# One attention-and-feed-forward kernel: a pinned TensorE order, a reordered first chunk, matmuls on zeros during the first loads, and a regrouped broadcast of the denominators

## The chip, the cores and the metric

The kernel runs on one core of one Trainium2 chip. The metric is device time in microseconds (us), smaller is better; a kernel is run several times and the median is quoted.

A ratio is the mean time of one kernel's runs over the mean of the other kernel's runs of the same rounds on the same chip, so it is not quite the ratio of the medians that stand beside it. Below 1 is faster than the kernel before.

Names used by the profile: PE is TensorE (matmuls), DVE is VectorE, ACT is ScalarE, POOL is GpSimd, SP the engine that issues most loads. A trailing "q" (ACTq, POOLq) is the sequencer of that engine, where it issues a DMA.

## The reference, cut to what matters

```python
def reference(A_x, A_wqkv, A_wo, B_x, B_w_gate, B_w_up, B_w_down, c, w_mod):
    # x: 1 x 2048 x 1024; 32 heads of 32; F = 3584; all bf16
    mod = (silu(c) @ w_mod)              # six rows of 1024: sa, ca, ga, sb, cb, gb
    h = layernorm(x) * (1 + ca) + sa
    q, k, v = heads(h @ wqkv)
    pq, pk = phi(q), phi(k)              # phi(t) = where(t > 0, t + 1, exp(t)) + 1e-6
    kv = einsum('bhsd,bhse->bhde', pk, v)
    z = einsum('bhsd->bhd', pk)
    den = einsum('bhqd,bhd->bhq', pq, z) + 1e-6
    o = einsum('bhqd,bhde->bhqe', pq, kv) / den
    x = x + ga * (o @ wo)
    h = layernorm(x) * (1 + cb) + sb
    return x + gb * ((silu(h @ w_gate) * (h @ w_up)) @ w_down)
```

The attention is linear. Every query needs only the sum over all keys (`kv`, `z`), so K and V of all tokens come before any output. Each query and head is divided by one number, `den`.

## The kernel before

The 2048 tokens are handled as four chunks of 512, called K0, V0, Q0 and so on below. A scheduler decides the order of instructions on each engine when the program is built, unless the program tells it otherwise; an engine then keeps to that order. The parts that the change and the argument touch:

```python
# loads, all issued by SP, in this order: c, four x tiles, then per half b of the contraction
for b in range(2):
    for q in (1, 0):
        t = big("wme", [DC, NB])                       # modulation weights of this half
        nc.sync.dma_start(out=t[:], in_=wm_v[:, :, q * D + b * NB:q * D + (b + 1) * NB])
    for i in range(2):
        nc.sync.dma_start(out=wk[b][:, 2 * i:2 * i + 2, :], in_=wqkv_v[...])
# ... cut: wv follows after K0, wq only in chunk 2 ...

def phi_to(dst, acc):                                  # evacuates one PSUM bank of K or Q
    e = ep.tile([P, NB], BF16, name="eb")
    nc.scalar.activation(out=e[:], in_=acc, func=ACT.Exp)
    nc.vector.tensor_scalar(out=e[:], in0=e[:], scalar1=1.0, scalar2=PHI_EPS, op0=ALU.min, op1=ALU.add)
    nc.vector.scalar_tensor_tensor(out=dst, in0=acc, scalar=0.0, in1=e[:], op0=ALU.max, op1=ALU.add)

def q_phase(sc, lo=0, hi=DC):
    for qc in range(lo, hi):
        acc = acc_a()                                  # one of four PSUM banks
        for cc in range(DC):
            nc.tensor.matmul(acc[:], lhsT=wq[...], rhs=hTs[sc][:, cc, :], ...)
        phi_to(pqs[sc][:, qc, :], acc[:])

def den_norm(sc):
    # ... cut: 32 small matmuls give den, VectorE takes its reciprocal rb (128 x 128),
    #     four small DMAs write rb to rden_dram ...
    rbc = big("rbc", [HG, SCW])                        # 128 x 8 x 512 bf16, 1 MB
    rv = rden_dram[sc].rearrange("(g h) t -> h g t", h=HPC)
    for h in range(HPC):                               # HPC = 4, DH = 32
        nc.gpsimd.dma_start(out=rbc[h * DH:(h + 1) * DH, :, :],
                            in_=rv[h].unsqueeze(0).to_broadcast([DH, HG, SCW]))

def den_apply(sc):
    for k in range(4):
        ks = slice(2 * k, 2 * k + 2)
        nc.vector.tensor_tensor(out=pq[:, ks, :], in0=pq[:, ks, :], in1=rbc[:, ks, :], op=ALU.mult)

# order: K0 V0 K1 KV0 K1 V1 ... K3 V3, then
q_phase(0, 0, 2); kv_phase(3); q_phase(0, 2, 8); q_phase(1, 0, 1)
den_norm(0); den_apply(0)
# ... cut: rest of Q1, four output tiles (a_ps), Q2, Q3, den_norm(1), den_norm(2) ...
# then per chunk: gate/up (wgu) and down (wd), with the next chunk's output tiles in between
```

The denominators go out to DRAM and come back as a broadcast: each of the 32 rows of one head position is written to 32 partitions. That is what `rbc` is.

## Time and profile before

| | before |
|---|---|
| median of 3 runs | 859.06 us (858.94 to 859.39) |
| span of the profiled run | 856.0 us |
| TensorE busy | 832.5 us, 97% |
| V of chunk 0 ends | 56.6 us |
| gate/up of chunk 0 starts | 229.8 us |

The head of the page of before: the span, TensorE's busy time, and the clock row (40 slices of the span, granted clock in tenths).

```profile
span 856.0 us, 10310 instructions
...
PE 832.5 (97%) x4236; PEld 383.4 (45%) x4236; DVE 322.1 (38%) x621; ACT 141.1 (16%) x239; POOL 45.4 (5%) x125
...
PEclk9999999999999999999999999999999999999999
```

TensorE bounds the kernel. What can be won is what it loses, most of it before 57 us. Next is the timeline of TensorE of before. Its columns are start, duration, engine, line, operation, output and inputs, count, and in brackets the idle time just before with what ended it.

```profile
10.36 1.89 PE L175 MATMUL tp<-ident,xn 128*128 128x128 bf16 x16 [10.36 <-DVE xn L166]
...
20.82 1.44 PE L237 MATMUL acc<-wk,hT 128*128 128x512 bf16 x3
22.91 1.02 PE L207 MATMUL mod_ps<-scT,wme 128*128 128x1 bf16 x32 [0.66 <-DMA wme<-in_w_mod_dram]
23.79 12.77 PE L237 MATMUL acc<-wk,hT 128*128 128x512 bf16 x45
37.70 3.61 PE L237 MATMUL acc<-wk,hT 128*128 128x512 bf16 x16 [1.14 <-DVE pk L222]
41.83 3.20 PE L251 MATMUL acc<-wv,hT 128*128 128x512 bf16 x14 [0.51 <-DMA wv<-in_A_wqkv_dram]
45.81 10.95 PE L251 MATMUL acc<-wv,hT 128*128 128x512 bf16 x50 [0.79 <-DMA wv<-in_A_wqkv_dram]
```

TensorE idles for 10 us, starts the first half of K only behind the second block of modulation matmuls, and later waits for wv. The K matmuls also run slowly at first. The following are the groups of the K line in two short stretches of before; the three durations are the shortest, median and longest in ns.

```profile
L237 PE MATMUL acc<-wk,hT x3: 587/634/634, 20.8 to 21.6; 128*128 128x512 bf16 x3
...
L237 PE MATMUL acc<-wk,hT x11: 379/379/380, 29.7 to 31.9; 128*128 128x512 bf16 x11
```

The same matmul lasts 634 ns at first and 379 ns from 29.7 us on: the array is cold, then warm. The clock row does not show it.

Three more views of before matter later; they show how the broadcast travels. First the tile view of `rbc`: the issues, and from issue to landing (shortest, median, longest).

```profile
L348 POOL DMA_DIRECT2D rbc<-rden_scratch x16: 583/588/622, 173.8 to 294.4; - x16
...
DMA to landing us min/median/max: 4.1/8.9/12.9
```

Then the table of windows while the first four broadcasts run. The last three columns are the granted clock, the mean busy share of the core's 16 DMA engines, and GB/s.

```profile
178.00:179.00 1.00, 1.00 (x6) 0.47 (x5) 0.60 (x1) 1.00 (x3) 0.00 (x0) 1.00 1.02 221
```

All 16 engines are busy. Last, the timeline of VectorE at the multiply that uses the broadcast.

```profile
186.86 2.49 DVE L356 TENSOR_TENSOR pq<-pq,rbc 128x1024 bf16<-128x1024 bf16 x4
```

The multiply at 186.86 has no wait in brackets. The data were there, and seven Q evacuations had been placed between the reciprocal (169.5 us) and this multiply.

### The profile page before, as it was taken

How to read it: one execution, taken by the hardware profiler on the slowest of the kernel's cores; microseconds unless marked ns; L12 is line 12 of the kernel's file. 1: busy time of each engine (PE TensorE's matmuls, PEld its weight loads, DVE VectorE, ACT ScalarE, POOL GpSimd, SP SyncE). 2: the span in 40 equal slices, each digit the busy share in tenths (PEclk: the TensorE clock that was granted, in tenths of full speed). 3: DMA queues.
4: the chain of work that ended last, by engine and by line, in shares of the span. 5: the costliest groups of instructions: out<-in, count | busy, mean ns of one | idle time of the engine just before them, and what ended most of it. 6: DMA issues, size and time to landing. Idle time of an engine off the chain costs nothing.

```text
span 856.0 us, 10310 instructions
## 1 busy us (share of the span) xinstructions
PE 832.5 (97%) x4236; PEld 383.4 (45%) x4236; DVE 322.1 (38%) x621; ACT 141.1 (16%) x239; POOL 45.4 (5%) x125
## 2 busy tenths in 40 slices
PE   3899999999999999999999999999999999999997
PEld 2344444544444444444444444444444444444443
DVE  5884532658613333542211155211224532211122
ACT  2223333351311110001111100011110001111000
POOL 2110000012210100100000011000000100000000
PEclk9999999999999999999999999999999999999999
DMA  9699900028995492738344073483503629720011
GB/s 302 232 218 303 319 6 1 1 51 222 297 249 175 120 337 66 222 90 258 122 140 155 1 215 106 145 267 104 165 32 103 186 87 294 234 80 1 18 56 38
DMA packets 126478, 128.72 MB, mean 150 GB/s; under 512 B 33632, under 2 KB 107488, under 8 KB 126432
## 3 DMA queue, kind: packets, MB, share of 16 engines
q1 hardware_dynamic: 122208, 115.36, 45.1%
q0 software_dynamic: 3840, 12.65, 4.7%
q8 instruction: 33, 0.54, 0.3%
q10 hardware_dynamic: 384, 0.07, 0.0%
q14 instruction: 13, 0.11, 0.0%
HBM read 108.01 MB, written 12.71 MB: 141 GB/s over the span
## 4 chain that ended last, share of the span: by engine, by line
PE 91%; DMA 3%; DVE 3%; SPq 2%; POOL 0%; issue 0%; ACT 0%; DVEq 0%; POOLq 0%
PE acc L464 45%; PE acc L484 23%; PE acc L251 6%; PE a_ps L428 5%; PE acc L237 5%; PE acc L262 5%; DMA wv<-in_A_wqkv_dram 1%; SPq L114 1%; DMA x_sb<-in_A_x_dram 1%; PE kvp L273 1%; SPq L110 1%; DMA x_scratch<-x_1999 1%; DVE xn L166 1%; DVE stats L162 0%; POOL rstd L156 0%; PE modr L298 0%
## 5 line engine op out<-in xcount | busy, mean ns | idle before, releaser
L464 PE MATMUL acc<-h2T,wgu 128*128 128x512 bf16 x1792 | 387.4, 379 | 0.0
L464 PEld LDWEIGHTS <-wgu 128*128 128x128 bf16 x1792 | 175.3, 98 | 211.3
L484 PE MATMUL acc<-wd,gu 128*128 128x512 bf16 x896 | 196.3, 379 | 0.0
L470 DVE TENSOR_TENSOR gu<-acc,e 128x512 bf16<-128x512 f32 x112 | 77.5, 692 | 299.0 <-PE acc L464 294.3
L469 ACT ACTIVATE e<-acc 128x512 f32<-128x512 f32 x112 | 66.8, 597 | 502.5 <-PE acc L464 502.5
L484 PEld LDWEIGHTS <-gu 128*128 128x128 bf16 x896 | 87.7, 98 | 105.7
L237 PE MATMUL acc<-wk,hT 128*128 128x512 bf16 x256 | 60.6, 395 | 1.1 <-DVE pk L222 1.1
L487 DVE TENSOR_TENSOR e<-acc,gb_bc 128x512 f32<-128x512 f32 x32 | 22.1, 692 | 104.2 <-PE acc L484 104.2
L262 PE MATMUL acc<-hT,wq 128*128 128x512 bf16 x256 | 57.2, 379 | 1.0 <-DVE pq L222 1.0
L428 PE MATMUL a_ps<-wo,pq 128*128 128x512 bf16 x256 | 57.8, 379 | 0.1
L251 PE MATMUL acc<-wv,hT 128*128 128x512 bf16 x256 | 56.1, 379 | 1.3 <-DMA wv<-in_A_wqkv_dram 1.3
L220 ACT ACTIVATE eb<-acc 128x512 bf16<-128x512 f32 x64 | 37.8, 598 | 100.9 <-PE acc L237 48.9
L221 DVE TENSOR_SCALAR eb<-eb 128x512 bf16<-128x512 bf16 x64 | 18.5, 294 | 61.6 <-ACT eb L220 61.4
L237 PEld LDWEIGHTS <-hT 128*128 128x128 bf16 x256 | 25.3, 101 | 32.8 <-issue 6.0
L251 PEld LDWEIGHTS <-hT 128*128 128x128 bf16 x256 | 25.0, 98 | 31.9 <-issue 1.1
L262 PEld LDWEIGHTS <-wq 128*128 128x128 bf16 x256 | 24.9, 98 | 30.7 <-issue 1.2
L428 PEld LDWEIGHTS <-pq 128*128 128x128 bf16 x256 | 24.8, 98 | 30.8 <-DVE pq L356 1.5
L254 ACT CAST v<-acc 128x512 bf16<-128x512 f32 x32 | 18.7, 585 | 37.8 <-PE acc L251 37.8
L489 DVE TENSOR_TENSOR ob<-e,x1r 128x512 bf16<-128x512 f32 x32 | 22.1, 692 | 1.1
L222 DVE SCALAR_TENSOR_TENSOR pq<-acc,eb 128x512 bf16<-128x512 f32 x32 | 21.9, 690 | 0.8
L162 DVE BATCH_NORM_STATS2 stats<-x_sb 128x6 f32<-128x512 bf16 x32 | 20.7, 668 | 4.0 <-DMA x_sb<-in_A_x_dram 4.0
L222 DVE SCALAR_TENSOR_TENSOR pk<-acc,eb 128x512 bf16<-128x512 f32 x32 | 21.7, 687 | 0.5
(130 smaller groups left out, 245.9 us busy)
## 6 DMA issues: line engine op xcount, KB each, us to landing
wgu<-in_B_w_gate_dram SPq DMA_DIRECT2D x28, 1024.0 KB, 6.4
wgu<-in_B_w_up_dram SPq DMA_DIRECT2D x28, 1024.0 KB, 8.9
x_sb<-in_A_x_dram SPq DMA_DIRECT2D x32, 256.0 KB, 5.0
wml<-in_w_mod_dram SPq DMA_DIRECT2D x8, 1024.0 KB, 9.8
x1r<-x_scratch SPq DMA_DIRECT2D x32, 256.0 KB, 3.0
wd<-in_B_w_down_dram SPq DMA_DIRECT2D x7, 1024.0 KB, 14.3
wme<-in_w_mod_dram SPq DMA_DIRECT2D x4, 1024.0 KB, 10.6
rbc<-rden_scratch POOLq DMA_DIRECT2D x16, 256.0 KB, 8.9
```

The source lines that it names most:

```text
L220: nc.scalar.activation(out=e[:], in_=acc, func=ACT.Exp)
L222: nc.vector.scalar_tensor_tensor(out=dst, in0=acc, scalar=0.0, in1=e[:], op0=ALU.max, op1=ALU.add)
L237: nc.tensor.matmul(acc[:], lhsT=hTs[sc][:, cc, t * P:(t + 1) * P], rhs=wk[cc // 4][:, cc % 4, nb * NB:(nb + 1) * NB], start=(cc == 0), sto ...
L251: nc.tensor.matmul(acc[:], lhsT=hTs[sc][:, cc, t * P:(t + 1) * P], rhs=wv[cc // 4][:, cc % 4, nb * NB:(nb + 1) * NB], start=(cc == 0), sto ...
L262: nc.tensor.matmul(acc[:], lhsT=wq[cc // 4][:, cc % 4, qc * P:(qc + 1) * P], rhs=hTs[sc][:, cc, :], start=(cc == 0), stop=(cc == DC - 1))
L428: nc.tensor.matmul(a_ps[:], lhsT=pq[:, hg, t * P:(t + 1) * P], rhs=wo[hg // 4][:, hg % 4, ns], start=(hg == 0), stop=(hg == HG - 1))
L464: mm = nc.tensor.matmul(acc[:], lhsT=w[:, cc, fj * P:(fj + 1) * P], rhs=h2Ts[sc][:, cc, :], start=(cc == 0), stop=(cc == DC - 1))
L469: nc.scalar.activation(out=sg[:], in_=ps[0][:], func=ACT.Silu)
L470: gm = nc.vector.tensor_tensor(out=guT[sc][f // GPT][:, f % GPT, :], in0=ps[1][:], in1=sg[:], op=ALU.mult)
L484: nc.tensor.matmul(y_ps[:], lhsT=guT[sc][f // GPT][:, f % GPT, t * P:(t + 1) * P], rhs=wd[f // WDF][:, f % WDF, ns], start=(f == 0), stop= ...
L487: nc.vector.tensor_tensor(out=yt[:], in0=y_ps[:], in1=gb_bc[:, ns], op=ALU.mult)
L489: nc.vector.tensor_tensor(out=ob[:], in0=yt[:], in1=x1r[:], op=ALU.add)
```

## The change

The intent is to fill the start. wv and wq are queued early, K0 is split by halves of the contraction so that its first half runs before the second modulation block, Q0 comes right after V0, and matmuls on a zero tile (48 of them, results never read) keep the array warm while loads arrive. TensorE's stream is pinned to the order of the program, so that the scheduler cannot undo this. Layer normalisation of the later chunks moves from VectorE to ScalarE, the x1 stores from GpSimd's queue to ScalarE's. Along with it, the four broadcasts of the denominators become one, with a new order of rows in the scratch buffer.

```diff
+    def mm(out, lhsT, rhs, start, stop):
+        return tc.keep_in_program_order(nc.tensor.matmul(out, lhsT=lhsT, rhs=rhs, start=start, stop=stop))
 # ... cut: every matmul and transpose goes through mm / transpose ...
+        if b == 0:
+            load_x(STC - 1, nc.sync)
+    wv = load_w(wqkv_v, 2 * D, "wv")
+    for st in range(STC, 2 * STC):
+        load_x(st, nc.sync)
+    wq = load_w(wqkv_v, 0, "wq")
 # ... cut ...
-                nc.gpsimd.memset(zmask[rs, hg, HPC * hg + h:HPC * hg + h + 1], 1.0)
+                nc.gpsimd.memset(zmask[rs, hg, HG * h + hg:HG * h + hg + 1], 1.0)
 # ... cut: normalise_act, ln1 and modulate split into parts ...
         rbc = big("rbc", [HG, SCW])
-        rv = rden_dram[sc].rearrange("(g h) t -> h g t", h=HPC)
-        for h in range(HPC):
-            nc.gpsimd.dma_start(out=rbc[h * DH:(h + 1) * DH, :, :],
-                                in_=rv[h].unsqueeze(0).to_broadcast([DH, HG, SCW]))
+        rv = rden_dram[sc].rearrange("(h g) t -> h (g t)", h=HPC)
+        nc.gpsimd.dma_start(out=rbc[:].rearrange("p g t -> p (g t)"),
+                            in_=rv.unsqueeze(1).to_broadcast([HPC, DH, HG * SCW]))
 # ... cut ...
+    def keep_warm(acc, n):
+        for _ in range(n):
+            mm(acc[:], lhsT=sel[:, 0, :], rhs=sel[:], start=True, stop=True)
+    keep_warm(accs[5], 26)
+    with in_order(nc.vector, nc.scalar, nc.gpsimd):
+        # ... cut: normalise and transpose tiles 0 to 2, keep_warm(accs[5], 4) after each ...
+        for b in range(2):
+            mod_block(b, 1)
+            keep_warm(idle, 2)
+            mod_block(b, 0)
+            keep_warm(idle, 3)
+            # ... cut: modulate ...
+            if b == 0:
+                k_mms(0, gs, accs, 0, 4)            # first half of the contraction
+                # ... cut: fourth tile ...
+            else:
+                k_mms(0, gs, accs, 4, 8)
 # ... cut ...
         v_phase(sc)
         if sc + 1 < NSC:
-            ln1(sc + 1, True)
-            modulate_all(hTs[sc + 1], ca1T, saT)
+            with tc.issue_after(last_on[nc.vector.engine]):
+                ln1(sc + 1)
+                modulate_all(hTs[sc + 1], ca1T, saT)
+        if sc == 0:
+            q_phase(0)
 # ... cut: the later Q chunks are redistributed, den_norm(1) moves ahead of the output tiles ...
-        nc.gpsimd.dma_start(out=x1_dram[st * P:(st + 1) * P, :], in_=x1[:])
+        nc.scalar.dma_start(out=x1_dram[st * P:(st + 1) * P, :], in_=x1[:])
```

## The prediction

> **What bounds the kernel.** TensorE: the header of the page has it busy 832.5 of 856.0 us. Counting its matmuls at the steady start-to-start spacing of the timeline (448 gate/up matmuls in 96.7 us, 0.216 us each) I get about 827 us of work; with 4.4 us of tail after the last matmul that leaves roughly 24 us that any reordering could win. The timeline of TensorE says where they are: the first transpose starts at 10.36 us, and V of chunk 0 ends at 56.6 us, when only about 35 us of that work is done: 21 us lost before 56.6, about 2.5 us after it (waits of 1.0 us at 215.6, 0.8 us at 229.6, and smaller ones).
>
> Three losses make up the first part that can move. (a) The first half of K (24 matmuls, 5.2 us warm) could run from about 16 us, when the first modulation blocks are in, but in the stream it stands behind the second block: only 3 K matmuls start before 23.8 us. (b) From 20.8 to 29.5 us the K matmuls last 634 ns each, later 379 ns: the array is cold. The Trainium skill, "TensorE: Matmul & The Clock Gate", Part 1, says that the clock is halved until about 3.4 us of sustained activity; the trace agrees (634 against 379 ns), although the page's PEclk row shows full clock. That costs about 2.7 us. (c) Stalls of 1.1 us at 37.7 (a PSUM bank not yet evacuated), and 0.5 and 0.8 us for wv, which was issued only at 36.45 us, behind x loads that waited for buffers, while the DMA row was nearly empty from 27 to 36 us.
>
> **What the change does.** wv and wq are queued right behind wk. With 350 to 380 GB/s wv lands near 31 us. The fourth x tile goes behind the first wk half. The last modulation block still lands at about 22.8 us, because the same bytes are ahead of it; this is the wall. After it: 32 small matmuls 0.9, copy and first modulate 0.5, so the second K half starts at about 24.5, ends at 29.7; the two remaining groups 3.5: K ends near 33.2 (41.3 before). V then needs 13.8 us: it ends at 47.0 instead of 56.6. Q0 follows with wq long present, while the normalisation of chunk 1 finishes near 53 us. The 48 zero matmuls lie in idle time, except about 0.6 us just before the second K half. So **-9.6 us**, all on the critical path.
>
> Q0 only moves, no work is saved. Later stalls: the two near 215 and 230 us go (-1.7); pinning removes the freedom to slip ready matmuls in front of waiting ones: I allow +1 to +2 us, at the transposes of KV (only 16 matmuls ahead of them), at the first attention-output tile (waits for the denominators' round trip, 20 us before, 19.6 us of work now), and at the first gate weights (19.6 us after the output tiles, 28 before). Normalisation moved to ScalarE is off the path.
>
> **Prediction: 849.0 us, range 846 to 852.5.** Faster by over 2% 0.03, within 2% 0.96, slower 0.01.
>
> **Right or wrong.** Timeline of TensorE: V of chunk 0 ends at 47 (45.5 to 49); K matmuls at 379 ns from the first; second K half starts at 24 to 25.5, set by the landing of the last modulation block; no wait for wv. Steady gate/up and down stretches unchanged. TensorE busy grows by the zero matmuls.
>
> **What would make it wrong.** Zero matmuls that do not keep the clock up, or that overrun the first transposes (26 cold ones could last to 9 us); a slower DMA start; head-of-line waits of several us at the three places above, since nothing can slip past them.

## The result, and the profile after

| | before | after |
|---|---|---|
| median of 4 runs each | 859.0 us (858.02 to 859.39) | 881.3 us (879.47 to 881.36) |
| ratio, 95% interval | | 1.0256 (1.0238 to 1.0274) |
| span of the profiled run | 856.0 | 879.6 |
| V of chunk 0 ends | 56.6 | 47.7 |
| gate/up of chunk 0 starts | 229.8 | 247.4 |
| gate/up of chunk 1 starts | 388.7 | 412.2 |

The changed kernel is slower by 2.6%. Up to V0 it is 8.9 us ahead; at the first gate/up matmul it is 17.6 us behind. Most of these 26.5 us are lost between 187 and 240 us. The head of the page of after:

```profile
span 879.6 us, 10369 instructions
...
PE 840.3 (96%) x4201; PEld 387.4 (44%) x4284; DVE 306.7 (35%) x602; ACT 173.9 (20%) x267; POOL 37.0 (4%) x124
...
PEclk9999999989799999999999999999999999999999
```

TensorE's busy time grew (zero matmuls, and matmuls on a cold array), and the clock row now dips in its 9th and 11th slices, that is from 176 to 198 and from 220 to 242 us. The timeline of TensorE of after:

```profile
1.21 8.33 PE L98 MATMUL acc<-sel 128*128 128x512 bf16 x26 [1.21 <-DVE sel L390]
...
16.22 5.35 PE L98 MATMUL acc<-wk,hT 128*128 128x512 bf16 x24
...
25.20 8.81 PE L98 MATMUL acc<-wk,hT 128*128 128x512 bf16 x39
33.84 13.98 PE L98 MATMUL acc<-wv,hT 128*128 128x512 bf16 x63
47.66 7.07 PE L98 MATMUL acc<-hT,wq 128*128 128x512 bf16 x31
57.61 8.73 PE L98 MATMUL acc<-hT,wq 128*128 128x512 bf16 x31 [2.88 <-DVE pq L262]
...
198.35 0.58 PE L98 MATMUL acc<-hT,wq 128*128 128x512 bf16 x1 [10.40 <-DVE pq L262]
...
201.34 13.98 PE L98 MATMUL a_ps<-wo,pq 128*128 128x512 bf16 x63
...
230.58 5.83 PE L98 MATMUL acc<-hT,wq 128*128 128x512 bf16 x16 [8.36 <-DVE pq L262]
238.15 3.61 PE L98 MATMUL acc<-hT,wq 128*128 128x512 bf16 x16 [1.74 <-DVE pq L262]
...
247.44 55.42 PE L98 MATMUL acc<-h2T,wgu 128*128 128x512 bf16 x251
```

The start is as intended: both halves of K and all of V run without a gap. Then there are four waits, all said to be for VectorE's evacuation of Q (`pq`): 2.88, 10.40, 8.36 and 1.74 us. The matmuls after the first three waits are cold (those after the last, 16 in 3.61 us, are not): the 32 after 57.61 (31 of them recorded) take 8.73 us where the 32 before took 7.07. Half clock shows in the windows of after for the long waits (0.50 in the stretch from 192 to 194 us).

Why was VectorE late with Q? Its own timeline of after answers for the 10.40 us:

```profile
179.31 0.69 DVE L262 SCALAR_TENSOR_TENSOR pq<-acc,eb 128x512 bf16<-128x512 f32 x1
194.87 2.50 DVE L388 TENSOR_TENSOR pq<-pq,rbc 128x1024 bf16<-128x1024 bf16 x4 [14.86 <-DMA rbc<-rden_scratch]
```

VectorE stands at the multiply for 14.86 us, waiting for the broadcast; the Q evacuations placed behind it in its stream cannot pass, the four PSUM banks of Q fill, and TensorE stands too. The tile view of `rbc` of after gives the transfer:

```profile
L380 POOL DMA_DIRECT2D rbc<-rden_scratch x4: 700/710/715, 175.5 to 310.3; - x4
...
DMA to landing us min/median/max: 19.3/23.8/29.0
```

and the windows of after give the load on the DMA engines while it runs:

```profile
182.00:184.00 2.00, 2.00 (x11) 0.90 (x10) 0.00 (x0) 1.68 (x4) 0.00 (x0) 1.00 0.25 61
```

One transfer of 1 MB takes 19.3 us at best, with a DMA share of 0.25. A quarter of 16 engines is four engines (the view gives only the mean share; that it is four fully busy ones is a reading, which e5 supports). In before the same megabyte went as four transfers with a share of about 1. The second wait has the same root, by a longer way. These are lines of the chain that ended last, in order of time: start, duration, what.

```profile
175.51 19.33 DMA rbc<-rden_scratch
...
211.59 15.71 DMA x1r<-x_scratch
...
227.38 0.33 ACTq L515
```

The second broadcast was issued at 205.4 us, right ahead of the x1 stores and the first x1 reload. That reload (256 KB) took 15.71 us, against a median of 3.0 in the same kernel. ScalarE's queue waited for it before it issued the fourth x1 store at 227.38, so ScalarE's Exp, and with it the Q evacuations, stood still. That is the 8.36 us.

### The profile page after: what moved, and what is told of

It is laid out like the page before. It is cut to its first block, busy times and chain, and to the rows that moved or that the text cites. A ratio compares the mean times of both kernels' runs of the same rounds, so it can differ in the third digit from the quotient of the medians. Undisturbed runs are those within 1.5% of the kernel's fastest.

```text
span 879.6 us, 10369 instructions
## 1 busy us (share of the span) xinstructions
PE 840.3 (96%) x4201; PEld 387.4 (44%) x4284; DVE 306.7 (35%) x602; ACT 173.9 (20%) x267; POOL 37.0 (4%) x124
## 4 chain that ended last, share of the span: by engine, by line
PE 82%; DMA 11%; DVE 4%; issue 1%; ACT 1%; POOL 1%; ACTq 0%; SPq 0%; DVEq 0%; POOLq 0%
PE acc L98 75%; DMA rbc<-rden_scratch 5%; PE a_ps L98 5%; DMA x1r<-x_scratch 2%; DMA wd<-in_B_w_down_dram 2%; DVE stats L198 1%; DVE pq L388 1%; DMA x_scratch<-x_2148 1%; DMA x_sb<-in_A_x_dram 1%; PE kvp L98 1%; DMA h2T<-xn 0%; DMA rden_scratch<-rb 0%; PE modr L98 0%; DVE pq L262 0%; ACT v L297 0%
## 5 line engine op out<-in xcount | busy, mean ns | idle before, releaser
L98 PE MATMUL acc<-hT,wq 128*128 128x512 bf16 x248 | 62.3, 403 | 24.1 <-DVE pq L262 23.4
L98 PE MATMUL acc<-wk,hT 128*128 128x512 bf16 x250 | 56.1, 379 | 0.3
L192 POOL TENSOR_TENSOR rstd<-veps,neg_half 128x1 f32<-128x1 f32 x32 | 17.9, 558 | 449.7 <-DVE veps L190 449.7
## 6 DMA issues: line engine op xcount, KB each, us to landing
wd<-in_B_w_down_dram SPq DMA_DIRECT2D x7, 1024.0 KB, 28.7
rbc<-rden_scratch POOLq DMA_DIRECT2D x4, 1024.0 KB, 23.8
```

The costliest lines, as they stand in the source:

```text
L98: return tc.keep_in_program_order(nc.tensor.matmul(out, lhsT=lhsT, rhs=rhs, start=start, stop=stop))
L192: nc.gpsimd.tensor_tensor(out=rstd[:, 0:n], in0=veps[:, 0:n], in1=neg_half[:].to_broadcast([P, n]), op=ALU.pow)
```

## The experiments

Each kernel is the changed kernel (after) with the edit shown, unless said otherwise. Medians are of four runs each. The kernel before, on the same chips, had medians of 858.07 (e1 to e4), 858.37 (e5 to e8) and 858.33 us (e9, e10).

The theory (A in the expectations): the single broadcast uses 4 of 16 DMA engines, lands late, and VectorE and ScalarE hold Q's evacuations behind it. It rests on the Trainium skill, "DMA: Bandwidth & Descriptors", section "Why a DMA increments its semaphore by 16 and not by 1" (the paragraph on how many engines): the number of engines is the largest number up to 16 that divides the size of the slowest dimension, other than 1, of both sides. The source is [4, 32, 4096] and the destination [128, 4096], so 4; in before it is 32 rows to 32 partitions, so 16. The trace agrees: share 0.25 against about 1. The rivals were: the x1 stores moved to ScalarE (theory B); the pin on TensorE (theory C); the fact that it is one transfer rather than four; the new 8 KB rows; and the place of the multiply in VectorE's stream. The normalisation moved to ScalarE was not tested by itself; e1 and e9 keep it and are fast, so it is not enough to cause the loss.

| run | edit in a few words | median us (range) | ratio (95%) |
|---|---|---|---|
| e1_rbc4 | broadcast as four | 853.52 (853.4–855.31) | 0.9951 (0.9936–0.9966) |
| e2_x1pool | x1 stores on GpSimd | 881.34 (879.87–881.9) | 1.0268 (1.0253–1.0283) |
| e3_rbc4_x1pool | both | 858.88 (857.55–861.37) | 1.0012 (0.9993–1.0032) |
| e4_nopin | no pin | 887.23 (884.98–890.44) | 1.033 (1.0306–1.0355) |
| e5_rbc_swap | one transfer, source dims swapped | 854.96 (852.47–857.55) | 0.9957 (0.9929–0.9985) |
| e6_late_apply | multiply placed later | 869.55 (868.48–869.88) | 1.0125 (1.011–1.014) |
| e7_before_rbc1 | before, with the one broadcast | 874.17 (871.29–875.04) | 1.0175 (1.0154–1.0196) |
| e8_rbc4_q0 | e1, Q0's evacuations first | 856.66 (854.61–859.65) | 0.9969 (0.9951–0.9987) |
| e9_rbc4_q0_wml | e8, and a load moved forward | 850.95 (850.93–851.06) | 0.9915 (0.9898–0.9932) |
| e10_rbc4_nowarm | e1 without zero matmuls | 855.13 (854.54–855.89) | 0.9964 (0.9949–0.9979) |

### e1_rbc4: the broadcast in four parts again

```diff
-        nc.gpsimd.dma_start(out=rbc[:].rearrange("p g t -> p (g t)"),
-                            in_=rv.unsqueeze(1).to_broadcast([HPC, DH, HG * SCW]))
+        for h in range(HPC):
+            nc.gpsimd.dma_start(out=rbc[h * DH:(h + 1) * DH, :, :].rearrange("p g t -> p (g t)"),
+                                in_=rv[h].unsqueeze(0).to_broadcast([DH, HG * SCW]))
```

> The changed kernel with the broadcast of the denominators' reciprocals cut into four transfers of 32 partitions each; the new scratch layout (whole 8 KB rows) stays. Theory A (the single transfer runs on 4 of the 16 DMA engines, because its source starts with a dimension of 4, and takes 19 to 29 us; VectorE waits for it in order, PSUM is not evacuated, TensorE stands): each landing falls to 10 us or less, the DMA row is near full while it runs, the TensorE waits of 10.4 us near 188, 8.4 and 1.7 near 222 to 238, 2.7 near 342 and 2.1 near 352 go, with their cold matmuls: 852 to 858 us. Theory B (x1 stores on ScalarE's queue block its Exp): near 188 us 10 us come back, those near 222 stay: about 869. Theory C (the pinned TensorE stream): 879 or little below.

853.52 us: 27.8 us less than after. The new layout with its 8 KB rows is kept, so the rows are not the cause. The parts of its broadcasts landed in 3.6 to 11.8 us. The window of e1 while they run:

```profile
178.00:179.00 1.00, 1.00 (x7) 0.43 (x5) 0.48 (x2) 1.00 (x3) 0.00 (x0) 1.00 0.96 205
```

The share is back at 0.96. 205 GB/s over 0.96 of 16 engines is 13 GB/s per busy engine; after's 61 GB/s over 0.25 of 16 is 15. Each engine moved as much as before; there were four times fewer of them. VectorE's order changed too, as the scheduler put the first multiply behind eight Q evacuations instead of four, where nothing is left to wait for:

```profile
188.49 2.49 DVE L389 TENSOR_TENSOR pq<-pq,rbc 128x1024 bf16<-128x1024 bf16 x4
```

So e1 alone does not separate the transfer from the order; e5 holds the order, and e6 changes only the order. The last of the four parts, issued at 176.5 us, landed within 6.0 us: an estimate from this is that even at the place that the multiply has in after (behind the fourth evacuation, which ends at 179.5 us in e1) it would have waited about 3 us, not 14.86.

All the long waits near 190 and 225 us are gone. In the timeline of TensorE of e1 the waits of over 1 us below are left from 50 us on; the line at 224.45 is the first gate/up matmul:

```profile
57.09 8.75 PE L98 MATMUL acc<-hT,wq 128*128 128x512 bf16 x32 [2.32 <-DVE pq L262]
...
215.15 3.61 PE L98 MATMUL acc<-hT,wq 128*128 128x512 bf16 x16 [1.06 <-DVE pq L262]
...
224.45 1.89 PE L98 MATMUL acc<-h2T,wgu 128*128 128x512 bf16 x8
228.04 53.70 PE L98 MATMUL acc<-h2T,wgu 128*128 128x512 bf16 x248 [1.71 <-DMA wgu<-in_B_w_up_dram]
```

By TensorE's timeline after is behind e1 by 12.1 us at the first output tile (201.34 against 189.23), 23.0 at the first gate/up matmul (247.44 against 224.45) and 26.4 at the end (879.6 against 853.2). Thus the two waits, with the cold matmuls after them, cost 12 and 11 us, and about 3.4 come later, in the gate/up and down matmuls of chunk 0 (164.8 us in after, 161.4 in e1). These are put down to the last two broadcasts: after has a wait of 2.68 us at 342.47 for VectorE and two for down weights, 0.50 and 1.57 (their median landing is 28.7 us, 14.3 in before). The profiled run of e1 is its slowest (855.31 us; the other three took 853.4 to 853.54), hence 26.4 here and 27.8 by the medians.

### e2_x1pool and e3_rbc4_x1pool: the x1 stores back on GpSimd

```diff
-        nc.scalar.dma_start(out=x1_dram[st * P:(st + 1) * P, :], in_=x1[:])
+        nc.gpsimd.dma_start(out=x1_dram[st * P:(st + 1) * P, :], in_=x1[:])
```

e2 is after with this edit, e3 is e1 with it.

> The changed kernel with the x1 stores issued from GpSimd again, as before the change; the single broadcast stays. Theory A: little, 876 to 882 us, since x1 stores only wait behind the slow broadcast; the wait near 222 may shrink, because ScalarE is no longer held by a store's issue. Theory B: the waits of TensorE from 222 to 240 (10 us and some 2 us of cold matmuls) go: about 868. Theory C: no change.

> Both edits of the two runs before. Theory A alone: same as the four transfers alone, 852 to 858 us. If theory B holds beside A, the gains add and this is about 10 us faster than the four transfers alone.

e2 is as slow as after: 881.34 us, with waits of 9.98 and 10.07 us in the same places. From its timeline of TensorE:

```profile
197.51 3.57 PE L98 MATMUL acc<-hT,wq 128*128 128x512 bf16 x8 [9.98 <-DVE pq L262]
...
232.04 7.00 PE L98 MATMUL acc<-hT,wq 128*128 128x512 bf16 x24 [10.07 <-DVE pq L262]
```

The first x1 store then took 18.45 us from issue to landing, on the same queue right behind the broadcast, and VectorE stood 14.26 us until it freed its x1 tile; the normalisation on ScalarE, and the Exp behind it, came late by that. So ScalarE's queue was the way by which the second wait came, not its cause. The Trainium skill, "DMA: Bandwidth & Descriptors", section "Issuing engines are not separate DMA queues", says that transfers of all issuing engines share the same 16 engines and interleave. The trace of after agrees: while GpSimd's second broadcast ran, a store from ScalarE's queue took up to 15.6 us and SyncE's reload 15.71. (e2 cannot show it by itself, since its stores follow the broadcast on one queue.) e3 is 5.4 us slower than e1, on the same chip. With the four broadcasts the stores belong on ScalarE, and that part of the change is good.

### e4_nopin: TensorE free

```diff
-        return tc.keep_in_program_order(nc.tensor.matmul(out, lhsT=lhsT, rhs=rhs, start=start, stop=stop))
+        return nc.tensor.matmul(out, lhsT=lhsT, rhs=rhs, start=start, stop=stop)
```

and the same for the transposes.

> The changed kernel without the pinning of matmuls and transposes to program order; everything else stays. Theory C (with a free order TensorE would have slipped ready matmuls into the gaps): 10 us or more come back, under 871. Theories A and B: at the waits near 188 and 222 all PSUM banks are full, so nothing could slip; 878 to 884 us, perhaps worse at the start, where the zero matmuls may be moved.

887.23 us, 5.9 slower than after. The timeline of TensorE of e4 shows why:

```profile
19.89 1.01 PE L98 MATMUL mod_ps<-scT,wme 128*128 128x1 bf16 x32 [4.13 <-DMA wme<-in_w_mod_dram]
20.76 7.42 PE L98 MATMUL acc<-wk,hT 128*128 128x512 bf16 x24
```

The scheduler put part of the second modulation block ahead of the first half of K, which could have run from about 16 us. TensorE waits 4.13 us for its weights, and K then runs cold (24 in 7.42 us instead of 5.35). V0 ends at 55.9 instead of 47.7 us. The long waits behind the broadcast stay (9.44 and 7.51 us). The pin does not cause the loss; it wins about 8 us at the start, of which about 6 are left at the end.

### e5_rbc_swap: one transfer, but another leading dimension

```diff
-                            in_=rv.unsqueeze(1).to_broadcast([HPC, DH, HG * SCW]))
+                            in_=rv.unsqueeze(0).to_broadcast([DH, HPC, HG * SCW]))
```

This maps rows to the wrong partitions. It is no valid kernel, although its output passed the numeric comparison, which therefore does not resolve this part. It moves the same bytes in one transfer, and leaves VectorE's order as it is in after, with four Q evacuations ahead of the multiply.

> The changed kernel, still one broadcast transfer of the same bytes in the same 8 KB rows, but with the two leading dimensions of the source swapped: 32 copies of 4 rows instead of 4 rows of 32 copies. The result is wrong on purpose (partition p gets the row p mod 4 instead of p div 32). If the number of DMA engines follows the leading dimension (4 before, now 16 of 32): DMA share near 1 while it runs, landing 4 to 12 us, and the time falls to 853 to 858 us as with four transfers. If it is slow because it is one transfer, or because of its 8 KB rows: 19 to 29 us to landing as in the changed kernel, and 879 to 882 us.

The window of e5 in which the broadcast runs, and the multiply in VectorE's timeline:

```profile
174.00:176.00 2.00, 2.00 (x11) 0.89 (x10) 0.98 (x2) 1.68 (x5) 0.00 (x0) 1.00 0.71 295
```

```profile
178.13 2.50 DVE L388 TENSOR_TENSOR pq<-pq,rbc 128x1024 bf16<-128x1024 bf16 x4 [0.51 <-DMA rbc<-rden_scratch]
```

854.96 us. Landing is 5.0 to 8.9 us instead of 19.3 to 29.0, and the wait of 14.86 us becomes 0.51. Neither the single transfer nor the early place of the multiply costs anything by itself; the leading dimension of the source does. That it does so by the number of engines is the theory's reading, which the shares bear out (0.25 in after, 0.71 in e5, 0.96 in e1). One more thing differs: 295 GB/s over 0.71 of 16 engines is 26 GB/s per busy engine, not 13 to 15. In e5 successive rows of the broadcast come from different source rows; in after and e1, from the same one. Whether that is the reason was not tested. It is not needed, as e1 has the low rate per engine, on a share of 0.96, and is as fast.

### e6_late_apply: slow broadcast kept, multiply moved behind the Q evacuations

```diff
     den_norm(0)
-    den_apply(0)
     q_phase(1, 4, 5)
 # ... cut ...
     q_phase(2, 4, 5)
+    with tc.issue_after(last_phi[0].ins):
+        den_apply(0)
```

> The changed kernel with the slow broadcast kept, but the first multiplication by it ordered on VectorE behind the evacuations of the Q groups instead of in front of five of them. If the 10.4 us at 188 are VectorE's order, they shrink to what the first output tile itself waits: the broadcast lands near 194.9, so TensorE starts the tile at 195.6 to 196 instead of 201.3, a gain of 4 to 6 us: 875 to 878 us. If only the landing mattered, no gain: 879 to 882.

869.55 us, a gain of 11.8 us on after, more than was expected. The timeline of TensorE of e6:

```profile
193.39 15.78 PE L98 MATMUL a_ps<-wo,pq 128*128 128x512 bf16 x63 [4.47 <-DVE pq L389]
...
221.39 8.67 PE L98 MATMUL acc<-hT,wq 128*128 128x512 bf16 x32 [5.32 <-DVE pq L262]
```

The 10.40 us wait became 4.47: now TensorE waits for the broadcast itself, at the output tile that really needs it. The expectation missed the second effect: the second broadcast is issued at 194.1 instead of 205.4 us, so the x1 reloads no longer meet it at full length (all of them land within 8.7 us), and the second wait shrinks to 5.32 us. In after, then, a good half of the first wait came from VectorE's order: work that needed nothing stood behind work that waited.

### e7_before_rbc1: the kernel before, with the one broadcast

```diff
-                nc.gpsimd.memset(zmask[rs, hg, HPC * hg + h:HPC * hg + h + 1], 1.0)
+                nc.gpsimd.memset(zmask[rs, hg, HG * h + hg:HG * h + hg + 1], 1.0)
 # ... cut ...
-        rv = rden_dram[sc].rearrange("(g h) t -> h g t", h=HPC)
-        for h in range(HPC):
-            nc.gpsimd.dma_start(out=rbc[h * DH:(h + 1) * DH, :, :],
-                                in_=rv[h].unsqueeze(0).to_broadcast([DH, HG, SCW]))
+        rv = rden_dram[sc].rearrange("(h g) t -> h (g t)", h=HPC)
+        nc.gpsimd.dma_start(out=rbc[:].rearrange("p g t -> p (g t)"),
+                            in_=rv.unsqueeze(1).to_broadcast([HPC, DH, HG * SCW]))
```

> The kernel before with only the single broadcast (and the scratch and mask layout that it needs). Theory A: that alone makes it slow: the transfer lands after about 19 us on a quarter of the DMA engines, the schedule puts the multiplication in front of four Q evacuations, and TensorE waits some 8 to 12 us near 188, with more at the later ones: 867 to 882 us. If the single broadcast only hurts with the new order and the pinned stream: 857 to 861.

874.17 us, 15.8 more than before. TensorE's timeline of e7, then VectorE's:

```profile
192.87 15.65 PE L427 MATMUL a_ps<-wo,pq 128*128 128x512 bf16 x63 [8.89 <-DVE pq L355]
```

```profile
192.11 2.50 DVE L355 TENSOR_TENSOR pq<-pq,rbc 128x1024 bf16<-128x1024 bf16 x4 [14.52 <-DMA rbc<-rden_scratch]
```

The edit alone makes the old kernel slower, without any pin, zero matmul or new order in the program; the scheduler did move the multiply forward, in front of four Q evacuations. It costs less than in after (15.8 against about 27). There is no second wait of 8 us: the second broadcast is issued at 233.1 us, behind the x1 stores, not just ahead of them.

### e8_rbc4_q0 and e9_rbc4_q0_wml: the 2.9 us in Q0

In after and e1, VectorE normalises and modulates chunk 1 in front of Q0's evacuations: it waits for x tiles (1.94 us at 50.8 in after), and the eight modulates run from 53.9 to 56.5 us, while Q0's banks are full. e8 is e1 with the modulate behind the fifth evacuation, and chunk 2's statistics behind the last:

```diff
-            with tc.issue_after(last_on[nc.vector.engine]):
+            with tc.issue_after(last_phi[0].ins if sc == 1 else last_on[nc.vector.engine]):
                 ln1(sc + 1)
-                modulate_all(hTs[sc + 1], ca1T, saT)
+                if sc > 0:
+                    modulate_all(hTs[sc + 1], ca1T, saT)
         if sc == 0:
-            q_phase(0)
+            q_phase(0, 0, 5)
+            with tc.issue_after(last_phi[0].ins):
+                modulate_all(hTs[1], ca1T, saT)
+            q_phase(0, 5, 8)
```

> The changed kernel with four broadcasts, and on VectorE the modulation of chunk 1 behind the fifth Q evacuation of chunk 0 and the statistics of chunk 2 behind the eighth, instead of in front of the first. If the wait of 2.3 us at 54.8 (and 1.8 us of cold matmuls after it) is VectorE holding back the evacuations of Q0, both go: K of chunk 1 starts at 61.6 instead of 65.7, the time is 849 to 850.5 us. If the wait is for something else, it stays: 853 to 854.

Q0 then runs unbroken in 13.98 us, but e8 is not faster than e1: 856.66 us. The modulation weights for the next rows (`wml`) were now issued behind the delayed transposes of chunk 2, and TensorE waited 2.59 us for them at 98.15 and ran cold after. In the profiled run the start was also late: V0 ended at 50.5 us, after a wait of 1.34 us for the last modulation block that e1 does not have. e9 issues the first four `wml` loads ahead of those transposes:

```diff
             q_phase(0, 5, 8)
+            wml_a = load_mod([2 * D, 2 * D + NB, 5 * D, 5 * D + NB])
 # ... cut ...
-            row = mod_rows([2 * D, 2 * D + NB, 5 * D, 5 * D + NB])
+            row = mod_rows(wml_a)
```

> The run with four broadcasts and Q0's evacuations first, with the four loads for the first row of modulation moved in front of the transposes of chunk 2 on the loading queue. In the run without this, Q0 ran unbroken, but the loads were issued at 75 to 88 us behind those transposes and TensorE waited 2.6 us for them at 95.6. If that was all that ate the gain: no wait there, and 849 to 851 us, faster than the four broadcasts alone (853.5). If the changed order on VectorE costs elsewhere too: 853 to 857.

850.95 us, the fastest kernel, ahead of both before and after. TensorE's timeline of e9:

```profile
47.81 13.98 PE L98 MATMUL acc<-hT,wq 128*128 128x512 bf16 x62
...
223.95 53.70 PE L98 MATMUL acc<-h2T,wgu 128*128 128x512 bf16 x243 [1.59 <-DMA wgu<-in_B_w_up_dram]
```

Its first gate/up matmul starts at 220.5 us, 4.0 ahead of e1: in these two profiled runs the stall in Q0 with its cold matmuls was worth about 4 us. By the medians e9 gains 2.6 (the profiled run of e1 is its slowest, by 1.8 us), and the two ran on different chips. A wait for gate weights at 223.95 is left.

### e10_rbc4_nowarm: e1 without the zero matmuls

```diff
     def keep_warm(acc, n):
-        for _ in range(n):
+        for _ in range(0):
```

> The run with four broadcasts without the 48 matmuls on a zero tile. If they keep the array's clock up and the clock matters: the first 24 K matmuls last 634 instead of 379 ns and take 10 instead of 5.3 us, so they end near 26.5 instead of 21.6; the second modulation block and the second K half follow later, and V of chunk 0 ends 3 to 5 us later: 856 to 859 us. If the clock came up without them, or the landing of the last modulation block hides it: 852 to 854.

855.13 us, 0.13% of the ratio above e1, about 1 us. The two were run on different chips, so this is not far above what such a comparison resolves. The start does show the effect of the zero matmuls. This is TensorE's timeline of e10:

```profile
16.95 6.45 PE L98 MATMUL acc<-wk,hT 128*128 128x512 bf16 x22 [0.22 <-issue]
```

These K matmuls last 631 ns up to about 19.9 us, and V0 ends at 50.8 instead of 47.7 us. But most of the 3 us do not reach the end: Q0, arriving later, waits 1.49 instead of 2.32 us, and its second half stays warm (7.07 us, not 8.75). The stall took back what the zero matmuls had won. What they would be worth in e9, which has no such stall, was not run.

## Why the prediction was wrong, point by point

- **Right: what bounds the kernel, and the start.** V0 was predicted to end at 47.0 us and ended at 47.7; the second half of K was predicted to start between 24 and 25.5 us and started at 25.20; K ran at 379 ns throughout; there was no wait for wv. ("Nearly empty from 27 to 36 us" was too strong: the DMA share in before is 0.13 from 27 to 30 us and 0.65 from 33 to 36.) The term of −9.6 us measured −8.9. Part of it (2.7 us in the prediction) rests on the cold clock of the Trainium skill, "TensorE: Matmul & The Clock Gate", Part 1, which the trace bears out (634 against 379 ns), and e10 shows it at work.
- **Partly right: the later stalls and the pin.** Of the two stalls that should go, the one near 230 us went, and one of 1.06 us at 215 us is there in e1. At the first gate weights, one of the three places of the allowance, e1 waits 1.71 us, which is the size that was allowed. e4 shows that the pin is no danger by itself: it helps.
- **Wrong, the step that failed: "I allow +1 to +2 us"** for waits that nothing can slip past. It measured about 30 us by the medians: 27.8 from the broadcast (after against e1; 26.4 by the spans of the profiled runs) and 2.6 from Q0 (e1 against e9; 4.1 by the spans). The prediction did name the place, "the first attention-output tile (waits for the denominators' round trip, 20 us before, 19.6 us of work now)", but it carried the round trip over from before as if unchanged. The diff replaced its four broadcasts by one, and the prediction never costed those lines. Their landing went from a median of 8.9 to 23.8 us (e7: the same lines alone cost 15.8 us in the old kernel). From the `den` matmuls to the landing of the first broadcast, the trip took 14.0 us in before (167.5 to 181.5) and 25.5 in after (169.4 to 194.8), against the 19.6 us of work that were to hide it (20.4 in e1, from 168.88 to 189.23). So the longer trip makes some 5 of the 10.40 us, and e6 leaves 4.47; the rest is VectorE's order.
- **Wrong in the same step: the waits were looked for on TensorE only.** VectorE and ScalarE run in their own fixed order too. The multiply held Q evacuations that did not need the broadcast (e6), and a store in ScalarE's queue held the Exp behind it (after, 227.38 us).
- **Wrong: "the normalisation of chunk 1 finishes near 53 us".** It ended at 56.5, and it mattered for another reason than the one given: it stood in front of Q0's evacuations on VectorE. That cost a wait of 2.9 us and 1.7 us of cold matmuls (8.73 against 7.07).
- Wrong: "Steady gate/up and down stretches unchanged." Those of chunk 0 took 164.8 us instead of 158.9 (161.4 in e1).
- The zero matmuls overran the first transposes as feared (first transpose at 9.38 us, 7.98 without them in e10). The last modulation block, which sets the second half of K, landed at 23.5 us in after and 22.6 in e10. An effect of the zero matmuls on it is not shown: with them it landed between 22.7 (e3) and 24.8 us (e8).

With both losses mended, e9 measured 850.95 us, inside the predicted range of 846 to 852.5. Most of the sum was sound; one term was far too small. The remaining 2 us were not tested. Some 2.4 us are lost after the first gate/up matmul: e9 is 9.3 us ahead of before there (220.5 against 229.8) and 6.9 at the end, and its wait of 1.59 us for gate weights near 224 us is the one long wait in between; the matmuls around it are warm (379 ns).

## What to carry to other kernels

When a diff merges several DMAs into one, read the leading dimension of both sides before counting it as the same transfer: here [4, 32, 4096] used 4 of 16 engines, and the DMA share in the windows (0.25 against 1) shows it at a glance. When TensorE waits "for VectorE", follow VectorE's own stream back: the evacuation was ready and stood behind an instruction that waited for a DMA. Fill and pin the start of a kernel, but check the first place after it where banks fill, since a stall of 2.9 us there cost another 1.7 us in cold matmuls.

## What the Trainium skill lacked or had wrong

- "DMA: Bandwidth & Descriptors", specifications: it gives about 27 GiB/s per engine, which is 29 GB/s. Here a broadcast from DRAM that repeats one source row moved 13 to 15 GB/s per busy engine (61 GB/s at share 0.25, 205 at 0.96), and one that changes its source row 26 (295 at 0.71). The page has no rate for broadcasts.
- The same page explains how many engines a transfer gets, and that an engine takes its queues in turn, but gives no figure for how much a long transfer on four of them delays the transfers of others: in after a reload of 256 KB took 15.7 us instead of 3.0, and the down weights landed in a median of 28.7 us instead of 14.3. x1 stores and two DMA transposes were under way beside that reload, but no gate weights (the next were issued at 232.7 us); how much of the 15.7 us is sharing those four engines was not separated.
- "TensorE: Matmul & The Clock Gate", Part 1: it gives about 3.4 us of sustained activity until full clock, and calls the window free-running, so that the count of cold matmuls varies. In after the matmuls behind the stall in Q0 were cold for 3.4 us (57.61 to 60.98), as stated, but the zero matmuls at the start for 5.1 us (1.21 to 6.31).
- No page that was read describes the clock row of this profile, or says that it can show full clock over a cold start (634 ns per matmul in before, row at 9), while it does show 0.50 in later stalls (after, 192 to 194 us).
